# Four units' values in one run of 64 matmuls over five PSUM banks, in a fused attention and feed-forward kernel

## The chip, the cores and the metric

One core of a Trainium2 chip runs the kernel. The metric is the device time of one execution in microseconds (us), the median of several runs.

## What is computed

Sliding-window attention over 8 batches of 8 heads, 576 positions and 64 values a head: each position sees those at most 32 away. Its result, 4608 rows of 512, goes through a feed-forward layer with a sigmoid GELU.

```python
scores = (1 / sqrt(D)) * q @ k.T            # per batch and head
mask = abs(pos[:, None] - pos[None, :]) <= 32
attn = softmax(where(mask, scores, -1e9))
x = (attn @ v).transpose(0, 2, 1, 3).reshape(4608, 512)
h = x @ w_in                                # 512 -> 2048
out = (h * sigmoid(1.702 * h)) @ w_out      # 2048 -> 512
```

## The kernel before

**Units and tiles.** The 4608 rows are 36 units of 128 rows; four units make a tile of 512 rows, so there are 9 tiles. A unit holds two blocks of 64 queries. Its scores are computed transposed (keys in partitions), exponentiated on ScalarE into `p`, and multiplied by a mask of ones and zeros (`band`, L303) on VectorE. `values` (L311) multiplies `p` by V: for each of 8 heads and 2 blocks one matmul with 64 columns of `p` as weights and 65 columns of V, the last of them ones, so that the row sum comes out beside the 64 values. The two blocks of a head go to the lower and upper 64 partitions. The V of the first block lies in `ve`, that of the second in `vo`, the same rows moved by 64 partitions, which GpSimd copies (`odd_v`, L213, two copies a unit). `norm` (L330) takes the reciprocals of the row sums and multiplies, out of PSUM into `x`; `x_T` (L344) transposes `x` into `xT`, by a DMA that SP issues, or by TensorE through PSUM where a tag is given.

**PSUM.** There are eight banks: `A`, `C`, `B`, `E`, `LA`, `LB`, and `t`, which is two. A unit's values take either `t` (one reciprocal and one product on VectorE for eight heads) or `A` and `C` (one each for four heads and four).

**The feed-forward layer** is computed with seven half-size products a layer instead of eight (Winograd's form of Strassen's scheme), so sums of `xT`, of the weights and of `g` (`x_sums`, `w1_sums`, `g_sums`) are formed on VectorE. A tile's first layer is four groups (`l1_group`, L459); each issues P1, P7, P6, P2, P5, P4 and P3 of four 256-wide matmuls, over banks A, C, B and E. Between them ScalarE copies A to B and C to an SBUF tile, VectorE adds B and that tile into E (L484, after P6) and into C (L490, after P5), and ScalarE applies the GELU (L471). P5 and P3 add into B, so they wait until the addition before them has read it. Because P4 adds onto what VectorE has written in E, all of that bank must have been written by TensorE before.

**The order is written out by hand.** Each engine runs its instructions in the order in which the program issues them. The second layer of the tile before is a list of single matmuls, `l2`, and `do(l2, n)` issues the next n as fillers; a group's fillers stand after P1, P7, P2 and P4, as many as `SHARES` gives in that order (`fill`). Some of them carry an addition or a copy on VectorE or ScalarE behind them, and every 56th a store. `side` issues one piece of VectorE's waiting list `dv` after each of the two additions of a group, and `fill(4)` the rest of the list.

**One tile.** `front(t)` (L757) issues the scores of the next tile's four units in two pairs, with 20 fillers between and 12 behind. `back(t)` (L785) issues the four groups n = 0 to 3. Ahead of a group come `turn` (L748: two DMA transposes of q and k on SP), `fetch` (L736: loads of q, k and V on the queue of GpSimd, called POOL) and `spread` (L744: the `vo` copies of a later unit). Before the change, groups 1 and 3 begin with values: a unit in A and C, then one in `t`, with their `norm` and `x_T`, and a few fillers (`AHEAD`). Two masks are issued in group 0, two in group 1, and the sums of `g` of a group one group later. Tile 2 has an order of its own, with four runs of 16 value matmuls; in tile 7 unit 34 is transposed on TensorE in the last `front`.

Of the kernel before, what the change touches and what calls it, by code (L numbers as in the profile page):

```python
# [15 lines left out]
F32 = mybir.dt.float32  # L16
BF16 = mybir.dt.bfloat16
F16 = mybir.dt.float16
# [8 lines left out]
class _Kernel:  # L27
# [55 lines left out]
    def setup(self):  # L83
        nc, cst = self.nc, self.cst
        self.ident = cst.tile([128, 128], BF16, name="ident")
        self.identh = cst.tile([128, 128], F16, name="identh")
        self.mask = cst.tile([128, 4, SQ], BF16, name="mask")
        self.bias = cst.tile([128, 512], BF16, name="bias")
        self.w1 = cst.tile([128, 4, self.DFF], F16, name="w1")
        self.w2 = cst.tile([128, 16, self.DM], F16, name="w2")  # L90
        self.a = {i: cst.tile([128, 2, 1024], F16, name=f"a{i}") for i in (1, 2, 3, 4)}
        self.b = {i: cst.tile([128, 8, 256], F16, name=f"b{i}") for i in (1, 2, 3, 4)}
        self.k_first = cst.tile([128, 4, 64], BF16, name="k_first")
        self.v_first = cst.tile([64, self.H, 66], BF16, name="v_first")
        self.ve = [cst.tile([128, self.H, 66], BF16, name=f"ve{i}") for i in range(9)]
        self.vo = [cst.tile([128, self.H, 66], BF16, name=f"vo{i}") for i in range(5)]
        self.spark = cst.tile([128, 1], F32, name="spark")

    def setup_mask(self):
# [106 lines left out]
    def load_v(self, u, which=slice(None)):  # L206
# [3 lines left out]
        for off, b, s, n in list(self.pieces(128 * u, 128))[which]:  # L210
            self.nc.gpsimd.dma_start(t[off:off + n, :, :self.D], self.v[b, :, s:s + n, :].rearrange("h s d -> s h d"))  # L211

    def odd_v(self, u, eng, parts=(0, 1)):  # L213

        vo = self.vo[u % (3 if u > 15 else 5)]
        nxt = self.v_first if u == self.NU - 1 else self.ve[(u + 1) % 9][0:64]

        def words(ap):
            return ap.rearrange("p h d -> p (h d)").bitcast(I32)

        for i in parts:
            eng.tensor_copy(*((words(vo[64:128]), words(self.ve[u % 9][64:128])), (words(vo[0:64]), words(nxt)))[i])  # L222
# [88 lines left out]
    def values(self, u, tag):  # L311

        D = self.D
        p = self.p.pop(u)
        if tag == "t":
            acc = self.bank(tag, name="pv")
            self.acc[u] = [acc]
            acc = [acc[:, 0], acc[:, 1]]
        else:
            acc = [self.bank(x, name="pv") for x in tag]  # L320
            self.acc[u] = [x.rearrange("p (b n) -> p b n", b=1) for x in acc]
        for h in range(self.H):
            o = slice((h % 4) * (D + 1), (h % 4 + 1) * (D + 1))
            for blk in range(2):
                vt = (self.ve[u % 9], self.vo[u % (3 if u > 15 else 5)])[blk]
                w = p[:, h % 2, h // 2 * 2 + blk, :] if len(p.shape) == 4 else p[:, h % 2, h // 4, h // 2 % 2, blk, :]
                self.mm(acc[h // 4][64 * blk:64 * blk + 64, o], w, vt[:, h, :D + 1],
                        start=(h % 4 == 0))

    def norm(self, u):  # L330
        dve, D = self.nc.vector, self.D
        x = self.x[u] = self.sb("x", [128, self.H, D], F16, 4)
        rec = self.sb("rec", [128, 2, 4, 1], F32, 3)
        at = 0
        for acc in self.acc.pop(u):
            n = acc.shape[1]
            acc = acc[:, :, 0:4 * (D + 1)].rearrange("p b (h e) -> p b h e", e=D + 1)
            r = rec[:, at:at + n]
            dve.reciprocal(r, acc[:, :, :, D:])
            dve.tensor_mul(x[:, 4 * at:4 * (at + n), :].rearrange("p (b h) d -> p b h d", b=n), acc[:, :, :, :D],  # L340
                           r.to_broadcast([128, n, 4, D]))
            at += n

    def x_T(self, u, tag=None, eng=None):  # L344
        nc = self.nc
        t, s = divmod(u, 4)
        if t not in self.xT:
            self.xT[t] = self.sb("xT", [128, 4, TILE], F16, 2)
        x = self.x.pop(u).rearrange("p h d -> p (h d)")
        out = self.xT[t][:, :, 128 * s:128 * s + 128]  # L350
        if tag is None:
            nc.sync.dma_start_transpose(out, x)
            return
        tp = self.bank(tag, [128, 4, 128], F16, "tp")
        for c in range(4):
            nc.tensor.transpose(tp[:, c, :], x[:, 128 * c:128 * c + 128], self.identh)  # L356
        self.copy(eng, out, tp)
# [186 lines left out]
    def layer2(self, pairs, last):  # L544
# [54 lines left out]
        for P in (6, 2, 4, 5, 3):  # L599
# [3 lines left out]

    SHARES = {("first", 1): (3, 0, 5, 4), ("first", 2): (0, 6, 6, 6), ("first", 3): (3, 1, 7, 7), ("last", 0): (0, 12, 6, 6),
              0: (4, 4, 6, 6), 1: (3, 3, 6, 6), 2: (0, 6, 5, 6), 3: (2, 2, 5, 5)}


    AHEAD = {1: (0, 6), 3: (2, 3)}  # L610

    def opening(self):

# [138 lines left out]
    @staticmethod  # L752
    def do(fs, n=99):
        for _ in range(min(n, len(fs))):
            fs.pop(0)()

    def front(self, t, late):  # L757

        l2, do = self.l2, self.do
        if t + 1 == self.NT:  # L760
            self.l2eng = self.nc.scalar
            do(late, 3)
            do(l2, 8)
            self.x_T(self.NU - 2, "t", self.l2eng)
            xs = self.x_sums(t)
            do(xs, 1)
            do(l2, 12)
            do(late)
            do(xs)
            return  # L770
        self.l2eng = self.nc.vector
        u = 4 * t + 4
        self.scores(u, "t")
        self.scores(u + 1, "AC")
        do(late, 2)
        do(l2, 20)
        do(late)
        xs = self.x_sums(t)
        do(xs, 1)
        self.scores(u + 2, "BE")  # L780
        self.scores(u + 3, "t")
        do(l2, 12)
        do(xs)

    def back(self, t):  # L785

        more = t + 1 < self.NT
        do, l2 = self.do, self.l2
        u = 4 * t + 4
        bands = [lambda i=i: self.band(u + i) for i in range(4)] if more else []  # L790
        dv = bands[0:2]
        for n in range(4):
            if (t, n) == (3, 1):
                self.turn(20)
            if (t, n) != (3, 0):
                self.turn(u + n + 4)
            if (t, n) not in ((2, 3), (3, 0), (3, 3)):
                self.fetch(u + n + 5)
            if t == 2 and n in (1, 3):
                self.values(u + n - 1, "t")  # L800
                self.norm(u + n - 1)
                self.x_T(u + n - 1)
            elif more and n in (1, 3):
                do(l2, self.AHEAD[n][0])
                self.values(u + n - 1, "AC")
                self.norm(u + n - 1)
                if u + n < self.NU - 1:
                    self.x_T(u + n - 1)
                self.values(u + n, "t")
                self.norm(u + n)  # L810
                self.x_T(u + n)
                do(l2, self.AHEAD[n][1])
            if (t, n) == (3, 0):
                self.fetch(20)
            self.spread(u + n + 2)
            if (t, n) == (3, 0):
                self.fetch(21)
            if (t, n) == (3, 3):
                self.fetch(24)

            key = ("first", n) if t == 2 else ("last", n) if not more else n
            share = dict(zip((1, 7, 2, 4), self.SHARES.get(key, (3, 3, 5, 5))))

            def fill(i):
                do(l2, share[i])
                self.l2eng = self.nc.scalar
                if t == 2 and n in (1, 3) and i == 7:
                    self.values(u + n, "t")
                    if n == 3:
                        self.norm(u + n)  # L830
                        self.x_T(u + n)
                if i == 4:
                    do(dv, 2 if (t, n) == (2, 2) else 99)

            def side(i):
                if (t, n, i) == (2, 1, 0):
                    self.norm(u + n)
                    self.x_T(u + n)
                else:
                    do(dv, 1)  # L840

            self.l1_group(t, n, fill, side)
            dv += bands[2:4] if n == int(t == 2) else []
            dv += self.g_sums(t, 2 * n, 2)
        return dv

# [131 lines left out]
```

## Time and profile before

| | |
|---|---|
| median of 3 runs (range) | 281.47 us (281.16 to 281.52) |
| the profiled execution | 281.27 us, of which its span 279.5 us |
| TensorE busy | 268.2 us (96% of the span) |
| VectorE busy | 210.9 us (75%) |
| ScalarE busy | 195.4 us (70%) |
| GpSimd busy | 133.0 us (48%) |
| granted TensorE clock | 0.999 |

The page calls TensorE PE, VectorE DVE, ScalarE ACT, GpSimd POOL, and the queue that issues DMAs SP. A row of a timeline gives the start in us from the span's start, the time from the first start to the last end, the engine, the source line, the operation, what is written and read, and how many instructions the row merges; in brackets stands idle time before it and what ended it. Matmuls overlap, so the cost of one is read from start to start, not from its duration.

### The profile page before, as it was taken

The numbers are of one execution on the slowest core, as the hardware profiler recorded it, in microseconds if no ns is written. First come the engines' busy times: TensorE is split into PE (matmuls) and PEld (weight loads), VectorE is DVE, ScalarE is ACT, GpSimd is POOL, SyncE is SP. The second block draws the span as 40 slices with busy tenths as digits, with TensorE's granted clock in tenths as the row PEclk, the third lists the DMA queues.
The fourth block names the chain that finished last, engine by engine and source line by source line (L and its number), as shares of the span: only waits on it lengthen the run. The fifth ranks groups of instructions, "written<-read, shape, count | busy, mean of one in ns | idle before, by whom it ended". The sixth has DMA issues, their size and how long they took to land.

```text
span 279.5 us, 8854 instructions
## 1 busy us (share of the span) xinstructions
PE 268.2 (96%) x3632; PEld 222.6 (80%) x3632; DVE 210.9 (75%) x491; ACT 195.4 (70%) x343; POOL 133.0 (48%) x199
## 2 busy tenths in 40 slices
PE   1989999999999999999999999999999999999995
PEld 1568656776888888888888888888888888888884
DVE  3454598897997798788888887888778887945731
ACT  2586893989897588758875877687759775568411
POOL 8894695999593554635684519442520100000000
PEclk9999999999999999999999999999999999999999
DMA  8999999999999999999999999999972050202023
GB/s 88 166 204 199 178 207 165 185 136 159 131 167 140 203 120 140 172 189 115 182 194 178 126 163 159 134 183 132 168 91 85 2 115 19 77 2 75 2 104 124
DMA packets 150265, 37.61 MB, mean 135 GB/s; under 512 B 138064, under 2 KB 145872, under 8 KB 150224
## 3 DMA queue, kind: packets, MB, share of 16 engines
q0 software_dynamic: 106656, 18.42, 95.5%
q1 hardware_dynamic: 43120, 18.10, 37.9%
q8 instruction: 28, 0.46, 0.7%
q10 hardware_dynamic: 448, 0.52, 0.6%
q14 instruction: 13, 0.11, 0.1%
HBM read 36.83 MB, written 9.44 MB: 166 GB/s over the span
## 4 chain that ended last, share of the span: by engine, by line
PE 90%; DMA 4%; POOL 3%; ACT 1%; issue 1%; POOLq 0%
PE o L70 41%; PE h L70 39%; PE pv L70 4%; DMA w<-in_moe_w_in_dram 4%; PE sc L70 3%; POOL ve L211 1%; POOL kq L152 1%; PE tp L201 1%; PE tp L244 1%; ACT p L279 1%; POOL w L125 1%; PE tp L368 0%; ACT kq L67 0%; PE tp L356 0%; ACT L692 0%
## 5 line engine op out<-in xcount | busy, mean ns | idle before, releaser
L471 ACT ACTIVATE g<-h 128x512 f16<-128x512 f32 x128 | 72.2, 598 | 35.0 <-PE h L70 34.8
L222 POOL COPY vo<-ve 64x264 int32<-64x264 int32 x71 | 32.7, 461 | 79.3 <-PE pv L70 52.0
L70 PEld LDWEIGHTS <-g 128*128 128x128 f16 x576 | 54.5, 98 | 10.1
L70 PE MATMUL h<-xs,a 128*128 128x256 f16 x384 | 57.6, 272 | 0.0
L70 PEld LDWEIGHTS <-a 128*128 128x128 f16 x512 | 49.5, 98 | 9.1
L70 PE MATMUL o<-w,g 128*128 128x256 f16 (+1 forms) x320 | 55.0, 294 | 0.0
L70 PEld LDWEIGHTS <-w 128*128 128x128 f16 x496 | 47.7, 98 | 7.6 <-DMA w<-in_moe_w_in_dram 0.2
L70 PE MATMUL h<-xT,w 128*128 128x256 f16 (+1 forms) x368 | 53.5, 277 | 0.1
L70 PEld LDWEIGHTS <-gs 128*128 128x128 f16 x384 | 36.7, 98 | 4.7
L70 PE MATMUL o<-b,g 128*128 128x256 f16 x256 | 38.3, 273 | 0.0
L70 PE MATMUL o<-b,gs 128*128 128x256 f16 x256 | 37.7, 273 | 0.0
L484 DVE TENSOR_TENSOR h<-h,s 128x512 f32<-128x512 f32 x32 | 22.4, 699 | 19.8 <-PE h L70 19.1
L211 POOL DMA_DIRECT2D ve<-in_v_dram x40 | 34.3, 864 | 5.6 <-DMA w<-in_moe_w_out_dram 2.1
L279 ACT ACTIVATE p<-sc 128x512 bf16<-128x512 f32 x64 | 32.8, 618 | 1.2 <-PE sc L70 1.0
L67 ACT COPY h<-h 128x512 f32<-128x512 f32 x32 | 18.8, 588 | 16.7 <-PE h L70 16.3
L340 DVE TENSOR_TENSOR x<-pv,rec 128x256 f16<-128x256 f32 (+1 forms) x52 | 27.4, 527 | 1.8
L141 POOL DMA_DIRECT2D qst<-in_q_dram x35 | 28.2, 809 | 0.3
L490 DVE TENSOR_TENSOR h<-h,s 128x512 f32<-128x512 f32 x32 | 22.4, 699 | 6.4 <-PE h L70 6.1
L141 POOL DMA_DIRECT2D kst<-in_k_dram x31 | 26.5, 855 | 0.8 <-DMA w<-in_moe_w_out_dram 0.8
L309 DVE TENSOR_TENSOR p<-p,mask 128x1024 bf16<-128x1024 bf16 x32 | 22.3, 696 | 0.2
L67 ACT COPY s<-h 128x512 f32<-128x512 f32 x32 | 19.2, 600 | 1.2
L70 PE MATMUL h<-xs,w 128*128 128x256 f16 x128 | 19.2, 273 | 0.0
(88 smaller groups left out, 343.2 us busy)
## 6 DMA issues: line engine op xcount, KB each, us to landing
out_dram<-o_sb SPq DMA_DIRECT2D x33, 256.0 KB, 4.6
ve<-in_v_dram POOLq DMA_DIRECT2D x32, 128.0 KB, 6.9
kst<-in_k_dram POOLq DMA_DIRECT2D x25, 128.0 KB, 6.5
qst<-in_q_dram POOLq DMA_DIRECT2D x21, 128.0 KB, 5.6
w<-in_moe_w_out_dram POOLq DMA_DIRECT2D x4, 512.0 KB, 11.0
w<-in_moe_w_in_dram POOLq DMA_DIRECT2D x3, 512.0 KB, 9.9
qst<-in_q_dram POOLq DMA_DIRECT2D x7, 96.0 KB, 5.7
kq<-in_q_dram POOLq DMA_DIRECT2D x2, 256.0 KB, 5.9
```

The lines of the kernel that those rows point to most:

```text
L67: (eng.copy if eng is self.nc.scalar else eng.tensor_copy)(out, in_)
L70: self.nc.tensor.matmul(out, lhsT, rhs, start=start, stop=stop, skip_group_check=True)
L125: self.nc.gpsimd.dma_start(self.w1[:, :, lo:lo + n], self.w_in[:, lo:lo + n].rearrange("(k p) f -> p k f", p=128))
L141: self.nc.gpsimd.dma_start(t[off:off + n], src[b, :, s:s + n, :].rearrange("h s d -> s h d"))
L211: self.nc.gpsimd.dma_start(t[off:off + n, :, :self.D], self.v[b, :, s:s + n, :].rearrange("h s d -> s h d"))
L222: eng.tensor_copy(*((words(vo[64:128]), words(self.ve[u % 9][64:128])), (words(vo[0:64]), words(nxt)))[i])
L279: self.nc.scalar.activation(p[:, eo].rearrange("k h s -> k (h s)"), sc[eo], AF.Exp, scale=self.scale)
L309: (eng or self.nc.vector).tensor_mul(pv, pv, msk.to_broadcast([128, 8, 2, SQ]))
L340: dve.tensor_mul(x[:, 4 * at:4 * (at + n), :].rearrange("p (b h) d -> p b h d", b=n), acc[:, :, :, :D], r.to_broadcast([128, n, 4, D]))
L471: act.activation(g[:, f, 256 * half:256 * half + 256], bank.rearrange("p (i n) -> p i n", i=2), AF.Gelu_apprx_sigmoid)
L484: dve.tensor_add(e, b, s7)
L490: dve.tensor_add(c, b, s7)
```

## The change

The four units of a tile are multiplied by V in one run at the start of group 2 (`values_four`). The 32 heads of the four units are laid one behind the other: seven into A, four into C, fourteen into the two banks of `t`, seven into E. E is filled from its end, and the first matmul of each half is 57 columns wider, so that the whole bank is written. `norm_four` then takes one reciprocal and one product for each of the four pieces, and issues the DMA transpose of each unit as soon as it is whole. `x` becomes one tile for four units (`xn`).

What stands around it moves: all four masks are issued in group 0 (two by `side`, two by `fill(4)`); the sums of `g` of group 0 are split in group 1, two ahead of P6 and one behind each addition; group 2 has nothing behind its first addition. The fillers are distributed anew (80 a tile as before, 64 in tile 2). `vo` has four buffers in rotation from unit 16 on instead of three. In tile 2, fetch 19 and turn 19 come a group sooner, and its order is that of the other tiles; unit 34 is no longer transposed on TensorE.

```diff
-        vo = self.vo[u % (3 if u > 15 else 5)]
+        vo = self.odd(u)                  # self.vo[u % 5 if u < 16 else (2, 3, 4, 0)[u % 4]]
...
+    FOUR = (("A", 0, 7), ("C", 7, 4), ("t", 11, 14), ("E", 25, 7))
+    def values_four(self, u):
+        D = self.D
+        p = [self.p.pop(u + i) for i in range(4)]
+        for tag, lo, n in self.FOUR:
+            acc = self.acc[u, tag] = self.bank(tag, name="pv")
+            b = [acc[:, i] for i in range(2)] if tag == "t" else [acc]
+            pad = 512 - 7 * (D + 1) if tag == "E" else 0
+            for i in range(n):
+                x, h = divmod(lo + i, self.H)
+                at, more = pad + i % 7 * (D + 1), pad * (i == 0)
+                for blk in range(2):
+                    vt = (self.ve[(u + x) % 9], self.odd(u + x))[blk].rearrange("p h d -> p (h d)")
+                    self.mm(b[i // 7][64 * blk:64 * blk + 64, at - more:at + D + 1], p[x][:, h % 2, h // 2 * 2 + blk, :],
+                            vt[:, h * (D + 2) - more:h * (D + 2) + D + 1], start=(i % 7 == 0))
+    def norm_four(self, u):
+        dve, D = self.nc.vector, self.D
+        x = self.xn.rearrange("p u h d -> p (u h) d")
+        done = 0
+        for tag, lo, n in self.FOUR:
+            m, at = min(n, 7), 512 - 7 * (D + 1) if tag == "E" else 0
+            acc = self.acc.pop((u, tag))
...
+            r = self.sb("rec4", [128, 2, 7, 1], F32, 3)[:, 0:n // m, 0:m]
+            dve.reciprocal(r, acc[:, :, :, D:])
+            dve.tensor_mul(x[:, lo:lo + n].rearrange("p (b h) d -> p b h d", b=n // m), acc[:, :, :, :D],
+                           r.to_broadcast([128, n // m, m, D]))
+            while 8 * (done + 1) <= lo + n:
+                self.x[u + done] = self.xn[:, done]
+                self.x_T(u + done)
+                done += 1
...
-    SHARES = {("first", 1): (3, 0, 5, 4), ("first", 2): (0, 6, 6, 6), ("first", 3): (3, 1, 7, 7), ("last", 0): (0, 12, 6, 6),
-              0: (4, 4, 6, 6), 1: (3, 3, 6, 6), 2: (0, 6, 5, 6), 3: (2, 2, 5, 5)}
-    AHEAD = {1: (0, 6), 3: (2, 3)}
+    SHARES = {("first", 0): (3, 3, 4, 4), ("first", 1): (3, 3, 4, 4), ("last", 0): (0, 12, 6, 6),
+              0: (4, 5, 6, 7), 1: (4, 5, 6, 7), 2: (2, 4, 4, 5), 3: (4, 5, 5, 6)}
...                                         # front, last tile
-            self.x_T(self.NU - 2, "t", self.l2eng)
...                                         # back
-        dv = bands[0:2]
+        dv = bands
...
+            if (t, n) == (2, 2):
+                self.turn(19)
...
+            if (t, n) == (2, 1):
+                self.fetch(19)
-            if t == 2 and n in (1, 3):
-                self.values(u + n - 1, "t")
-                self.norm(u + n - 1)
-                self.x_T(u + n - 1)
-            elif more and n in (1, 3):
-                do(l2, self.AHEAD[n][0])
-                self.values(u + n - 1, "AC")
...
+            if more and n == 2:
+                self.values_four(u)
+                self.norm_four(u)
+                do(l2, 1)
...
-                if i == 4:
-                    do(dv, 2 if (t, n) == (2, 2) else 99)
+                if i == 4 or more and (n, i) == (1, 7):
+                    do(dv, 99 if i == 4 else 2)
...
-                if (t, n, i) == (2, 1, 0):
-                    self.norm(u + n)
-                    self.x_T(u + n)
-                else:
+                if not (more and n == 2 and i == 0):
                     do(dv, 1)
             self.l1_group(t, n, fill, side)
-            dv += bands[2:4] if n == int(t == 2) else []
             dv += self.g_sums(t, 2 * n, 2)
```

More of the change, by code (lines that the diff above doesn't have):

```diff
@@ L96, in setup @@
         self.vo = [cst.tile([128, self.H, 66], BF16, name=f"vo{i}") for i in range(5)]
+        self.xn = cst.tile([128, 4, self.H, self.D], F16, name="xn")
         self.spark = cst.tile([128, 1], F32, name="spark")
@@ L211, in load_v, with odd @@
             self.nc.gpsimd.dma_start(t[off:off + n, :, :self.D], self.v[b, :, s:s + n, :].rearrange("h s d -> s h d"))
+    def odd(self, u):
+        return self.vo[u % 5 if u < 16 else (2, 3, 4, 0)[u % 4]]
     def odd_v(self, u, eng, parts=(0, 1)):
-        vo = self.vo[u % (3 if u > 15 else 5)]
+        vo = self.odd(u)
         nxt = self.v_first if u == self.NU - 1 else self.ve[(u + 1) % 9][0:64]
@@ L324, in values @@
             for blk in range(2):
-                vt = (self.ve[u % 9], self.vo[u % (3 if u > 15 else 5)])[blk]
+                vt = (self.ve[u % 9], self.odd(u))[blk]
                 w = p[:, h % 2, h // 2 * 2 + blk, :] if len(p.shape) == 4 else p[:, h % 2, h // 4, h // 2 % 2, blk, :]
@@ L331, in norm @@
         dve, D = self.nc.vector, self.D
-        x = self.x[u] = self.sb("x", [128, self.H, D], F16, 4)
+        x = self.x[u] = self.xn[:, u % 4]
         rec = self.sb("rec", [128, 2, 4, 1], F32, 3)
@@ L342, in norm @@
             at += n
+    FOUR = (("A", 0, 7), ("C", 7, 4), ("t", 11, 14), ("E", 25, 7))
[20 more added lines that the diff above has]
+            acc = self.acc.pop((u, tag))
+            if tag != "t":
+                acc = acc.rearrange("p (b n) -> p b n", b=1)
+            acc = acc[:, :, at:at + m * (D + 1)].rearrange("p b (h e) -> p b h e", e=D + 1)
+            r = self.sb("rec4", [128, 2, 7, 1], F32, 3)[:, 0:n // m, 0:m]
[6 more added lines that the diff above has]
+                done += 1
     def x_T(self, u, tag=None, eng=None):
@@ L794, in back @@
                 self.turn(20)
-            if (t, n) != (3, 0):
+            if (t, n) not in ((2, 3), (3, 0)):
                 self.turn(u + n + 4)
-            if (t, n) not in ((2, 3), (3, 0), (3, 3)):
+            if (t, n) == (2, 2):
+                self.turn(19)
+            if (t, n) not in ((2, 2), (2, 3), (3, 0), (3, 3)):
                 self.fetch(u + n + 5)
-            if t == 2 and n in (1, 3):
-                self.values(u + n - 1, "t")
-                self.norm(u + n - 1)
-                self.x_T(u + n - 1)
-            elif more and n in (1, 3):
-                do(l2, self.AHEAD[n][0])
-                self.values(u + n - 1, "AC")
[L806 to L809, printed above, removed]
-                self.norm(u + n)
-                self.x_T(u + n)
-                do(l2, self.AHEAD[n][1])
+            if (t, n) == (2, 1):
[4 more added lines that the diff above has]
+                do(l2, 1)
             if (t, n) == (3, 0):
@@ L819, in back @@
                 self.fetch(24)
-            key = ("first", n) if t == 2 else ("last", n) if not more else n
+            key = n if more else ("last", n)
+            if t == 2:
+                key = ("first", n) if n < 2 else n
             share = dict(zip((1, 7, 2, 4), self.SHARES.get(key, (3, 3, 5, 5))))
@@ L826, in fill @@
                 self.l2eng = self.nc.scalar
[L827 to L831, printed above, removed]
-                if i == 4:
-                    do(dv, 2 if (t, n) == (2, 2) else 99)
+                if i == 4 or more and (n, i) == (1, 7):
+                    do(dv, 99 if i == 4 else 2)
             def side(i):
-                if (t, n, i) == (2, 1, 0):
-                    self.norm(u + n)
-                    self.x_T(u + n)
-                else:
+                if not (more and n == 2 and i == 0):
                     do(dv, 1)
             self.l1_group(t, n, fill, side)
-            dv += bands[2:4] if n == int(t == 2) else []
             dv += self.g_sums(t, 2 * n, 2)
```

## The prediction

> **What bounds the kernel now.** I read the page first, then the chain that ended last, then the timelines of TensorE, VectorE and the SP queue over one tile, then the landing times of the transposes.
>
> ```profile
> span 279.5 us, 8854 instructions
> ...
> PE 90%; DMA 4%; POOL 3%; ACT 1%; issue 1%; POOLq 0%
> ```
>
> The profiled execution took 281.27 us: its span of 279.5 and 1.77 around it. The median of the three runs, 281.47, lies 0.20 above it. Differences are worked out on the former and added to the latter. 90% of the chain is TensorE, so only what shortens or stops its stream counts. Its timeline in tile 4 shows how little there is to take:
>
> ```profile
> 137.70 0.60 PE L70 MATMUL h<-xT,a 128*128 128x256 f16 x4
> ...
> 138.89 0.83 PE L70 MATMUL o<-w,g 128*128 128x256 f16 x6
> 139.55 0.60 PE L70 MATMUL h<-xT,w 128*128 128x256 f16 x4
> ...
> 149.53 0.38 PE L70 MATMUL o<-b,g 128*128 128x256 f16 x2
> ...
> 150.61 0.50 PE L70 MATMUL o<-b,g 128*128 128x256 f16 x3
> ```
>
> From 138.89 to 139.55 six matmuls start, so a 256-wide matmul costs 0.109 us. Two runs of 32 value matmuls lie in the gaps: from 137.70 + 4 x 0.109 = 138.14 to 138.89 is 0.75, and from 149.53 + 2 x 0.109 = 149.75 to 150.61 is 0.86. Together 1.61 us of a tile.
>
> **The run of 64.** Tile 2 has four runs of 16 instead, of which two consecutive rows (value rows between them left out) show the price:
>
> ```profile
> 83.30 0.60 PE L70 MATMUL h<-xT,a 128*128 128x256 f16 x4
> ...
> 84.21 0.61 PE L70 MATMUL h<-xT,w 128*128 128x256 f16 x4
> ```
>
> 84.21 - 83.30 - 0.44 = 0.47 for 16. So 16 further value matmuls cost 0.75 - 0.47 = 0.28, 0.0175 each, and the rest is the price of entering and leaving. One run of 64 is 0.75 + 32 x 0.0175 = 1.31; the two padded matmuls (122 columns for 65) add at most their share of a second matmul each, I take 0.03: 1.34. If nothing waited, a tile would gain 0.27.
>
> **What VectorE does after it.** All four normalisations now stand in front of group 2's first addition (E = B + s7), on one in-order engine:
>
> ```profile
> 138.59 0.18 DVE L339 RECIPROCAL rec<-pv 128x4 f32<-128x4 f32 x1 [0.16 <-PE pv L70]
> 138.81 0.42 DVE L340 TENSOR_TENSOR x<-pv,rec 128x256 f16<-128x256 f32 x1
> 139.15 0.17 DVE L339 RECIPROCAL rec<-pv 128x4 f32<-128x4 f32 x1
> 139.36 0.43 DVE L340 TENSOR_TENSOR x<-pv,rec 128x256 f16<-128x256 f32 x1
> 139.70 0.20 DVE L339 RECIPROCAL rec<-pv 128x8 f32<-128x8 f32 x1
> 139.93 0.69 DVE L340 TENSOR_TENSOR x<-pv,rec 128x512 f16<-128x512 f32 x1
> ```
>
> Start to start a reciprocal of 4 costs 0.21, of 8 0.23; a product of 256 costs 0.34 (it lasts 0.42), and 512 lasts 0.27 longer, 1.04 ns an element. So 448 wide costs 0.54, 896 wide 1.01, and reciprocals of 7 and 14 some 0.23 and 0.27. The new order A (7 heads), C (4), t (14), E (7) is 0.23 + 0.54 + 0.21 + 0.34 + 0.27 + 1.01 + 0.23 + 0.54 = 3.37 us. Two units take 1.95 now (138.59 to 139.93 + 0.61); twice that less two reciprocals (0.42) and the fixed 0.07 of two products is 3.34, so the slope holds together. With whole durations it would be 3.54, the bound above.
>
> Call the first value matmul V. The first reciprocal began 0.36 after V (138.23) for 8 matmuls; for 14 it is 0.46. VectorE is then free at V + 0.46 + 3.37 = 3.83. What the addition costs TensorE is seen in group 2 now:
>
> ```profile
> 146.10 0.60 PE L70 MATMUL h<-xs,a 128*128 128x256 f16 x4
> ...
> 147.56 0.60 PE L70 MATMUL h<-xs,a 128*128 128x256 f16 x4
> ```
> ```profile
> 146.81 0.70 DVE L484 TENSOR_TENSOR h<-h,s 128x512 f32<-128x512 f32 x1
> ```
>
> P6 starts at 146.10, the addition 0.71 later, lasts 0.70, and P5, which adds into the bank that it reads, starts 0.05 behind it: 1.46 at least, where P6, P2 and 5 fillers give 13 x 0.109 = 1.42. So 0.04 is lost now, in group 3 likewise; the tile loses 1.61 + 0.08 = 1.69 to values and these waits.
>
> After the change P5 of group 2 can start at V + 3.83 + 0.70 + 0.05 = 4.58. TensorE would be there at V + 1.25 (the run less its 0.09 of entry) + 27 matmuls (1 filler, P1 4, 2, P7 4, 4, P6 4, P2 4, 4) x 0.109 = 4.20. It waits 0.38. P1 needs only A's product and is not late (V + 1.37). With group 3's 0.04 (5 fillers) the tile loses 1.34 + 0.38 + 0.04 = 1.76, against 1.69: **+0.07, five tiles +0.35**. The 0.27 of the longer run is eaten by the longer normalisation.
>
> The Trainium skill says on the page TensorEngine Tiling (Array Packing), section PSUM Bottleneck, that tiling speeds up TensorE and not the emptying of PSUM, which may then bind; by it the run's gain goes as above, and without it a tile would gain 0.31 instead.
>
> Tile 2 loses 4 x 0.47 = 1.88 and some such waits (0 to 0.3) now; after it 1.76 and, in its groups 0 and 1 with 4 fillers (12 x 0.109 = 1.31 for 1.46), 0.15 each: 2.06, and perhaps as much again behind P5. I take +0.1 (-0.1 to +0.4). Unit 34's transposes leave TensorE before the last tile:
>
> ```profile
> 239.36 0.39 PE L356 MATMUL tp<-identh,x 128*128 128x128 f16 x4
> 239.58 0.60 PE L70 MATMUL o<-w,gs 128*128 128x256 f16 x4
> ```
>
> That is **-0.22**. So far +0.35 + 0.1 - 0.22 = **+0.23**.
>
> **At nothing:** masks and sums of g only change place on VectorE. In group 0 three masks now follow the second addition:
>
> ```profile
> L309 DVE TENSOR_TENSOR p<-p,mask 128x1024 bf16<-128x1024 bf16 x32 | 22.3, 696 | 0.2
> ```
>
> Counted from start to start, 0.08 less than they last, that addition, the masks, a quarter's output and two sums of g take 0.62 + 3 x 0.61 + 0.34 + 0.8 = 3.6 us from P5's end, 4.2 from its start; group 1's addition waits for P6, 36 matmuls later, and 0.71: 4.6. That hides them by 0.4 us; without it the excess is paid, at most 0.5 a tile. Fetch 19 keeps its place among POOL's instructions. The copies into vo wait for TensorE less with four buffers:
>
> ```profile
> POOL vo L222 <- PE pv L70: 52.0, 11, 14.1
> ```
>
> This idle time is on no chain. What comes next is the landing of V, and loads that go out sooner, beside the transposes.
>
> **What is moved on SP.** Four x transposes now go out together in group 2, ahead of the last q and k transposes of the tile (group 3's turn). Now:
>
> ```profile
> 143.25 0.81 SPq L505 DMA_DIRECT2D out_dram<-o_sb  x2
> 144.16 1.44 SPq L235 DMA_TRANSPOSE qT<-qst  x1
> 145.70 1.73 SPq L235 DMA_TRANSPOSE kT<-kst  x1
> 147.54 1.26 SPq L235 DMA_TRANSPOSE qT<-qst  x1
> 148.90 1.21 SPq L235 DMA_TRANSPOSE kT<-kst  x1
> 151.42 2.54 SPq L352 DMA_TRANSPOSE xT<-x  x2
> ```
>
> After the change the store of group 1 goes out about V - 1.4 (its last matmul is 20 before the run, then a copy), the next transposes at V - 0.5, and one follows another every 1.3 to 1.6 us (1.27 for the pair of x, 1.58 on average over 144.16 to 148.90), say 1.4: q, k, four x, q, k. The last, k of the next tile's last unit, starts at V - 0.5 + 7 x 1.4 = V + 9.3. It lands so long after:
>
> ```profile
> L235 SPq DMA_TRANSPOSE kT<-kst x18: 1192/1266/1992, 82.0 to 192.8; - x18
> ...
> DMA to landing us min/median/max: 2.4/6.0/8.8
> ```
>
> The median gives V + 15.3. The scores that read it come in the next front:
>
> ```profile
> 156.36 2.29 PE o L70 x20
> 158.65 0.63 PE sc L70 x32
> ```
>
> From P5 at V + 4.58: 17 matmuls (1.86), group 3's 48 (5.24) and 0.04, 0.09 and 0.63 for two units' scores, 2.29 for 20 fillers and 0.3 for the unit before: V + 15.0. So TensorE waits **0.33**, and everything on it is queued behind. Bounds: a landing of 5 costs nothing; one of 7.0, the median of two k transposes that went out among loads in tile 4 (131.8 to 137 us), costs 1.3.
>
> ```profile
> kT<-kst SPq DMA_TRANSPOSE x2, 7.0
> ```
>
> I take the median of the same kind. This happens behind tiles 3, 4 and 5: in tile 2 the change puts turn 19 ahead of the x transposes, and behind tile 6 there is no next k and the loads are over. 3 x 0.33 = **+1.0**. There the x transposes have two more, 2.8 us, before them; the sums of x that read them come some 14.7 us after V, the last goes out by V + 9.3 and lands about V + 15.3, where VectorE would wait first, TensorE only if that wait outlasts the 12 fillers and P1 (1.7 us): I take nothing, at most 0.5 once. The sum is +0.23 + 1.0 = +1.2: 282.5 beside the profiled 281.27, and **282.7** beside the median.
>
> **The rivals.** *The transposes land in time.* Until now the last k starts at 148.90 and is read at 158.9, 10 us later; then it has 5.7, and it misses by a third of a microsecond in my sum; a spacing of 1.3 alone wins 0.7. Then +0.23: 281.7, within the noise. Against it: x transposes and loads sooner share the engines.
>
> *VectorE does not bind the run (faster).* If the normalisation took 0.3 us less, or E's part did not stand before the addition, P5 would be held only by its own 1.46: 1.25 + 15 x 0.109 + 1.46 = V + 4.35, 0.23 sooner in six tiles: 0.23 - 1.4 = -1.2, 280.3. It decides once the chain is below 3.1. For it: the products of 448 and 896 stand in no row. Against it: their slope does.
>
> *Every VectorE instruction costs its whole duration.* The rows show the next one starting 0.08 before a product's end. If the wide ones with their reciprocals did not overlap, the chain would be 3.54, P5 0.17 later in six tiles: 0.23 + 1.0, 282.7. The Trainium skill, VectorE: DVE Perf Modes, section The DRAIN you can't avoid, says the next operation cannot issue until the pipeline is empty; the rows (0.34 from start to start for 0.42) speak against counting it so.
>
> **How the numbers follow.** About 0.2% (0.56 us) is what a measurement of this kernel can tell from no change. Late transposes have 0.46 (slower); transposes in time 0.28 (within); VectorE not binding 0.20 (faster); whole durations 0.06 (slower). Faster 0.20, within 0.28, slower 0.52. The forecast's own range is 282.0 to 285.6 (landings of 5.8 to 7.0). Leaving out the faster half of the faster case and the last of the late one, the range is 280.4 to 284.8.
>
> **What would show it.** In the changed profile: one run of 64 value matmuls a tile, about 1.3 us with its edges; the first DVE L484-type addition of group 2 about 3.8 after V with no idle time before it, and P5 at V + 4.6; TensorE stopping before the second unit of the second pair of scores behind tiles 3 to 5, released by the DMA of kT or qT; no x transposes on TensorE behind tile 7. I am wrong if the scores never wait (then 281.7), or if P5 starts right behind its fillers (then faster).

## The result, and the profile after

| | before | after |
|---|---|---|
| median (range), 6 runs each | 281.50 us (280.77 to 283.48) | 290.97 us (290.51 to 293.71) |
| profiled execution, its span | 281.27, 279.5 us | 291.84, 290.1 us |
| granted TensorE clock | 0.999 | 0.988 |

The change makes the kernel slower: the ratio is 1.034 (95% interval 1.029 to 1.039). The forecast, 282.7 us, had the direction and the place, not the size: its range ended at 284.8. The span grew by 10.6 us.

The page of after: the granted clock in 40 slices (tenths of full speed), and the chain that ended last, by engine and by line.

```profile
PEclk9999999999999999997799999999999999999999
...
PE 78%; DMA 13%; POOL 3%; DVE 2%; ACT 1%; issue 1%; DVEq 0%; POOLq 0%
```

DMA has 13% of the chain where it had 4%, and two slices in the middle have a lower clock; before, all forty read 9. The waits of TensorE (line, what it waited for: us in total, times, longest) name the DMA:

```profile
PE h L70 <- DVE h L526: 2.5, 6, 0.4
PE sc L70 <- DMA qT<-qst: 2.4, 1, 2.4
PE sc L70 <- DMA kT<-kst: 2.2, 3, 1.1
```

None of the three was there before. L526 is group 2's first addition, seen six times, once a run of 64. The other two are the scores behind tiles 3, 4 and 5. TensorE's timeline at these three fronts:

```profile
132.10 0.45 PE L70 MATMUL sc<-qT,kT 64*64 64x64 bf16 x24
134.97 0.31 PE L70 MATMUL sc<-qT,kT 64*64 64x64 bf16 x2 [2.43 <-DMA qT<-qst]
135.65 0.64 PE L70 MATMUL sc<-qT,kT 64*64 64x64 bf16 x22 [0.36 <-DMA kT<-kst]
136.22 1.89 PE L70 MATMUL o<-b,gs 128*128 128x256 f16 x8
137.90 1.06 PE L70 MATMUL o<-w,g 128*128 128x256 f16 x4
...
141.31 0.72 PE L70 MATMUL o<-b,g 128*128 128x256 f16 x5
...
165.97 0.48 PE L70 MATMUL sc<-qT,kT 64*64 64x64 bf16 x26
...
167.90 0.83 PE L70 MATMUL o<-b,gs 128*128 128x256 f16 x6
...
195.17 0.48 PE L70 MATMUL sc<-qT,kT 64*64 64x64 bf16 x26
...
196.73 0.72 PE L70 MATMUL o<-b,gs 128*128 128x256 f16 x5
```

The second pair of scores took 0.63 us before. Here it takes 136.22 - 132.10 = 4.12, then 1.93 and 1.56: 3.49, 1.30 and 0.93 us too long, **5.7 in all**. Behind the first of them the matmuls are slow: eight in 137.90 - 136.22 = 1.68 us, 0.21 each where 0.109 is the rule. The windows view (length, busy time of each engine, granted clock) of that stretch:

```profile
136.20:141.30 5.10, 5.10 (x28) 3.63 (x25) 2.03 (x5) 1.66 (x3) 2.22 (x3) 0.50 2.24 183
```

A clock of 0.50 for 5.1 us (from 132.0 to 136.2 it is 0.80 on average, so it falls at about 136.2 - 2 x 0.20 x 4.2 = 134.5, within the stop): 24 matmuls from 136.22 to 141.31 cost 5.09 us in place of 2.62, **2.5 us** more. This split is that of the profiled execution: over the six, the granted clock lies between 0.988 and 0.998. The remaining 10.6 - 5.7 - 2.5 = **2.4 us** are spread over the tiles; the largest part of them is a longer wait at P5 of group 2. VectorE in tile 3:

```profile
117.61 0.21 DVE L378 RECIPROCAL rec<-pv 128x7 f32<-128x7 f32 x1
117.86 0.62 DVE L379 TENSOR_TENSOR xn<-pv,rec 128x448 f16<-128x448 f32 x1
118.40 0.17 DVE L378 RECIPROCAL rec<-pv 128x4 f32<-128x4 f32 x1
...
119.21 1.09 DVE L379 TENSOR_TENSOR xn<-pv,rec 128x896 f16<-128x896 f32 x1
120.22 0.20 DVE L378 RECIPROCAL rec<-pv 128x7 f32<-128x7 f32 x1
120.45 0.62 DVE L379 TENSOR_TENSOR xn<-pv,rec 128x448 f16<-128x448 f32 x1
121.21 0.70 DVE L526 TENSOR_TENSOR h<-h,s 128x512 f32<-128x512 f32 x1
```

and TensorE there (the first value matmul, V, started at 117.16; the rows between are left out):

```profile
116.63 0.60 PE L70 MATMUL h<-xT,a 128*128 128x256 f16 x4
...
118.33 0.28 PE L70 MATMUL o<-b,gs 128*128 128x256 f16 x1
118.54 0.61 PE L70 MATMUL h<-xT,w 128*128 128x256 f16 x4
...
121.06 0.49 PE L70 MATMUL o<-w,g 128*128 128x256 f16 x3
121.96 0.60 PE L70 MATMUL h<-xs,a 128*128 128x256 f16 x4 [0.41 <-DVE h L526]
```

The run costs 118.33 - 116.63 - 0.44 = 1.26 us with its edges. P1 starts 0.21 behind one filler, so it waits 0.10. P5 starts at 121.96, where TensorE was done with its fillers at 121.06 + 3 x 0.109 = 121.39: it waits 0.57. (The 0.41 in the row is counted from the end of the last matmul, which lies past its slot.)

### The profile page after: what moved, and what is told of

It is laid out like the page before. It is cut to its first block, busy times and chain, and to the rows that moved or that the text cites. A ratio compares the mean times of both kernels' runs of the same rounds, so it can differ in the third digit from the quotient of the medians.

```text
span 290.1 us, 8830 instructions
## 1 busy us (share of the span) xinstructions
PE 270.7 (93%) x3628; PEld 224.0 (77%) x3628; DVE 210.6 (73%) x471; ACT 196.5 (68%) x342; POOL 133.0 (46%) x199
## 4 chain that ended last, share of the span: by engine, by line
PE 78%; DMA 13%; POOL 3%; DVE 2%; ACT 1%; issue 1%; DVEq 0%; POOLq 0%
PE h L70 36%; PE o L70 34%; DMA kT<-kst 8%; PE pv L70 3%; DMA w<-in_moe_w_in_dram 3%; DMA xT<-xn 2%; PE sc L70 2%; DVE h L526 1%; POOL ve L212 1%; POOL kq L153 1%; PE tp L202 1%; PE tp L248 1%; ACT p L283 1%; POOL w L126 1%; PE tp L410 0%
## 5 line engine op out<-in xcount | busy, mean ns | idle before, releaser
L70 PEld LDWEIGHTS <-g 128*128 128x128 f16 x576 | 55.8, 99 | 10.4
L70 PE MATMUL o<-w,g 128*128 128x256 f16 (+1 forms) x320 | 56.7, 298 | 0.0
L70 PE MATMUL o<-b,gs 128*128 128x256 f16 x256 | 40.7, 278 | 0.0
L526 DVE TENSOR_TENSOR h<-h,s 128x512 f32<-128x512 f32 x32 | 22.4, 699 | 21.1 <-PE h L70 19.5
L70 PE MATMUL o<-b,g 128*128 128x256 f16 x256 | 36.3, 273 | 0.0
L67 ACT COPY h<-h 128x512 f32<-128x512 f32 x32 | 18.5, 578 | 16.2 <-PE h L70 15.7
L313 DVE TENSOR_TENSOR p<-p,mask 128x1024 bf16<-128x1024 bf16 x32 | 21.4, 685 | 0.3 <-ACT p L283 0.3
L67 ACT COPY o_sb<-o 128x256 f32<-128x256 f32 (+1 forms) x23 | 10.7, 467 | 12.6 <-PE o L70 12.6
```

The lines of the kernel that those rows point to most:

```text
L67: (eng.copy if eng is self.nc.scalar else eng.tensor_copy)(out, in_)
L70: self.nc.tensor.matmul(out, lhsT, rhs, start=start, stop=stop, skip_group_check=True)
L313: (eng or self.nc.vector).tensor_mul(pv, pv, msk.to_broadcast([128, 8, 2, SQ]))
L526: dve.tensor_add(e, b, s7)
```

## Experiments

Two things could make the transposes late: the **order** on SP (the last two of q and k now go out behind four of x) and **crowding** (loads that GpSimd issues sooner, now that `vo` has four buffers, run beside them). And P5's longer wait could come from the length of VectorE's chain or from the addition waiting for E. Each kernel ran in alternation with the kernel before on one chip; ratios are to that. Kernels that share an edit name the one on which they stand.

**The turn first.** The changed kernel; the last turn of the tile goes out in group 2, ahead of the x transposes:

```diff
-            if (t, n) not in ((2, 3), (3, 0)):
+            if (t, n) != (3, 0) and not (more and n == 3):
                 self.turn(u + n + 4)
...
+            if more and n == 2:
+                self.turn(u + 7)
             if more and n == 2:
                 self.values_four(u)
```

> The changed kernel, but each tile's last two q and k transposes (group 3's turn) go out on SP ahead of the four x transposes instead of behind them. Theory A (the order on SP makes the next tile's scores wait, and the pause of 3.5 us in tile 4 halves TensorE's clock for some 5 us): the waits of 3.49, 1.30 and 0.93 us before the scores and the 2.5 us of slow matmuls all go, 290.97 - 8.2 = 282.8 us, granted clock 0.999. Theory B (loads that go out sooner and the x transposes crowd the DMA engines, whatever the order): the transposes still land late, waits of 1 us and more remain, 286 us or more.

Measured: 284.28 us, ratio 1.0075 (1.0042 to 1.0109). The scores behind the tile run through, and the clock is 0.998:

```profile
131.08 0.70 PE L70 MATMUL sc<-qT,kT 64*64 64x64 bf16 x48
131.71 1.05 PE L70 MATMUL o<-b,gs 128*128 128x256 f16 x8
```

The 48 take 0.63 again. So the order is needed for the late scores, and both they and the slow clock go with it. The six waits at P5 stay. By its ratio it is some 0.8 us slower than expected (1.0075 for 282.8 / 281.5 = 1.0046); a stop of 0.6 us before P1 of tile 4, where x, now last on SP, comes late, is part of that.

**The order alone.** The kernel before; from tile 3 on, group 3's turn goes out behind the x transposes of that group:

```diff
-            if (t, n) != (3, 0):
+            late = t > 2 and more and n == 3
+            if (t, n) != (3, 0) and not late:
                 self.turn(u + n + 4)
...
                 do(l2, self.AHEAD[n][1])
+            if late:
+                self.turn(u + 7)
```

> The kernel before, with one thing of the change alone: from tile 3 on, group 3's turn goes out on SP behind that group's two x transposes instead of ahead of them. Theory A: the last k transpose starts some 4 us later than now, lands about 160 instead of 154 us in tile 4, and the scores that read it (about 159) wait 0.5 to 1.5 us behind tiles 3 to 5: 283 to 286 us. Theory B: without the four x transposes in a row and without sooner loads nothing is late, 281.5 us.

Measured: 302.0 us, ratio 1.0675 (1.0593 to 1.0758), far more than expected. Its waits of TensorE, and the clock of one of three such stretches of 6.8 us:

```profile
PE sc L70 <- DMA qT<-qst: 7.8, 3, 3.5
PE sc L70 <- DMA kT<-kst: 5.0, 3, 1.8
```
```profile
134.80:141.60 6.80, 5.16 (x45) 3.71 (x46) 1.61 (x4) 1.66 (x3) 1.89 (x3) 0.50 1.92 191
```

The new order, with the loads issued when they were before, is enough to make the scores wait, here longer than in the changed kernel, since in group 3 the x transposes themselves wait for the values: the k transpose starts at 128.13 for scores at 131.2. What I undershot is how fast the price grows: a stop of this length brings the half clock.

This run does not separate order from crowding, though. GpSimd issues six loads from 123.69 to 128.96 us here, as it does before (123.74 to 129.01). Before, the last k transpose of the tile left at 121.17, ahead of them; here it leaves at 128.13, behind them. It lands so long after, before and here:

```profile
kT<-kst SPq DMA_TRANSPOSE x1, 4.3
```
```profile
kT<-kst SPq DMA_TRANSPOSE x1, 8.6
```

Moving a transpose back on SP thus made it later twice: it left 7 us later, and it stood among loads that had not moved.

**E ahead of t.** The kernel with the turn first, and E's seven heads are filled and normalised before t's fourteen, whose normalisation goes behind group 2's second addition:

```diff
-    FOUR = (("A", 0, 7), ("C", 7, 4), ("t", 11, 14), ("E", 25, 7))
+    FOUR = (("A", 0, 7), ("C", 7, 4), ("E", 11, 7), ("t", 18, 14))
...
-                self.norm_four(u)
+                self.norm_four(u, "ACE")
...
+                if more and (n, i) == (2, 1):
+                    self.norm_four(u, "t")
```

> As e1, and E is filled and normalised before t; t's normalisation is issued behind group 2's second addition instead of ahead of the first. Theory C (P5 of group 2 waits 0.58 us because the first addition writes E and so stands behind the whole chain of four normalisations, and does not overlap E's product): the addition starts 0.71 after P6, P5 waits 0.15 (4 fillers instead of 5.4), six tiles save 0.43 each: 2.6 us less than e1, about 280.2. Rival D (the addition is held by P2, after whose last matmul it also started): P5 still waits 0.5 or more, same as e1.

Measured: 281.94 us, ratio 0.9993 (0.9966 to 1.0021). VectorE and TensorE of that place:

```profile
119.54 0.70 DVE L528 TENSOR_TENSOR h<-h,s 128x512 f32<-128x512 f32 x1 [0.97 <-PE h L70]
```
```profile
119.83 0.49 PE L70 MATMUL o<-w,g 128*128 128x256 f16 x3
120.30 0.60 PE L70 MATMUL h<-xs,a 128*128 128x256 f16 x4
```

The addition now waits for P6 and not for VectorE, and P5 starts 0.47 after the last three fillers started: it waits 0.14 in place of 0.57, six times, 2.6 us in sum, close to the 2.3 us that the median fell. VectorE's chain in front of the addition was the cause of these 0.43 us a tile; the 0.14 left is the addition waiting for P6. The rival that P2 holds the addition falls too: P2, started at 119.29, ran until 119.89.

**The fillers.** The kernel with E ahead of t, and the fillers moved to where 0.14, 0.10 and 0.04 were still lost:

```diff
-    SHARES = {("first", 0): (3, 3, 4, 4), ("first", 1): (3, 3, 4, 4), ...
-              0: (4, 5, 6, 7), 1: (4, 5, 6, 7), 2: (2, 4, 4, 5), 3: (4, 5, 5, 6)}
+    SHARES = {("first", 0): (2, 2, 5, 5), ("first", 1): (2, 2, 5, 5), ...
+              0: (4, 5, 6, 7), 1: (4, 5, 6, 7), 2: (2, 2, 6, 5), 3: (3, 4, 6, 6)}
...
-                do(l2, 1)
+                do(l2, 2)
```

> As e3, and the 36 fillers of groups 2 and 3 are dealt out so that 2 follow the run (instead of 1) and 6 stand between P2 and P5 in both groups (instead of 4 and 5); tile 2's groups 0 and 1 get 5 there and 5 behind P4 (instead of 4 and 4). By the arithmetic 'P5 can start 1.46 us, 13.4 matmuls, after P6' the waits of 0.14, 0.09 and 0.04 in six tiles go (1.6 us), and 0.35 in tile 2: about 1.9 us less than e3, 280.0 us, or 0.5% below the kernel before. If the fillers only move the wait to P3 or to the next group's P1, the time stays that of e3, 281.9.

Measured: 282.11 us (279.88 to 288.39), ratio 1.0002 (0.9971 to 1.0033): by its time, neither the gain nor its absence is shown. In the profiled execution (284.13 us) the small waits are gone, but TensorE stops once, for 2.7 us before P7 of tile 4's first group, for sums of x that wait for the x transposes; 3.4 us at half clock follow:

```profile
PE h L70 <- DVE xs L444: 2.8, 2, 2.5
```

So what is left there is x, last on SP with loads beside it. That its lateness changes from run to run fits the wide spread of the times, but only this execution has a profile.

**Without the late loads of V.** The changed kernel, turn not moved; V of the units from 22 on is not loaded, and an older V is multiplied instead:

```diff
-        elif u >= 18:
+        elif 18 <= u < 23:
             self.load_v(u - 1)
```

> The changed kernel without the loads of V from unit 22 on (those units' values are computed from old V): a third of the loads beside the transposes of tiles 4 and 5 is gone, the order on SP is the changed kernel's. Theory A (order alone): the last k transpose still starts some 10 us after the run of values and lands 5 to 6 us later: waits of about 0.3 to 1 us before the scores stay, 3 us in all, 287 to 289 us. Theory B (crowding): waits behind tiles 4 and 5 vanish, 284 to 286 us.

Measured: 288.24 us, ratio 1.0217 (1.0146 to 1.0289). The scores behind tile 3 stop for 2.0 us in place of 3.5, behind tile 4 not at all, behind tile 5 for 0.9 (the rows of the first stand in the last section).

With a third of the loads gone, half of the waiting goes. So crowding has a share in it, and the order another: behind tile 3 the last k goes out 5.7 us before it is read in place of 4.9, and lands after 7.6 us in place of 8.1. As this kernel also moves less data altogether, it does not settle the shares.

**Loads staggered, turn first.** The fillers' kernel; from tile 4 on the `vo` copies of group 0 go ahead of its loads on GpSimd, which holds the loads back until V has landed:

```diff
+            if n == 0 and t > 3:
+                self.spread(u + 2)
             if (t, n) not in ((2, 2), (2, 3), (3, 0), (3, 3)):
                 self.fetch(u + n + 5)
...
-            self.spread(u + n + 2)
+            if n > 0 or t < 4:
+                self.spread(u + n + 2)
```

> As e4, and from tile 4 on GpSimd copies vo before it issues group 0's loads, so that these go out some 6 us later, when the copies' V has landed, and not among the transposes that follow the run. If loads crowd the transposes of x (whose landing made VectorE wait up to 1.5 us and TensorE's P1 0.6 us in e1 and e3), that wait goes in the tiles from 5 on: up to 0.7 us less than e4. If not, the same as e4; if POOL now brings V late to the run, slower by a microsecond or more.

Measured: 278.93 us, ratio **0.991** (0.988 to 0.994): 0.9% faster than the kernel before. Its span is 277.2 us, DMA has 5% of its chain, and its waits of TensorE are those of the opening and of the last unit's transposes, which the kernel before has too: none for the transposes of a later tile, none at P5.

**Turns in group 1 instead.** The fillers' kernel; from tile 4 on the turns of groups 2 and 3 and a fetch go out in group 1:

```diff
+            if early and n == 1:
+                self.fetch(u + 7)
+                self.turn(u + 6)
...
-            if more and n == 2:
+            if more and n == (1 if early else 2):
                 self.turn(u + 7)
```

> As e4, and from tile 4 on the tile's last four q and k transposes go out on SP in group 1, ahead of the store there (which waits for ScalarE until some 1.4 us before the run), so that the x transposes are first on SP after the run. The x transposes then start up to 3 us sooner than in e1 and e3; if their queue place is what makes x late, no wait of TensorE before P1 remains in tiles 5 to 8: 0.7 us less than e4. If crowding alone does it, the same as e4.

Measured: 281.05 us, ratio 0.9973 (0.9949 to 0.9997). That interval overlaps the one of the fillers' kernel (0.9971 to 1.0033), so a gain from moving the turns is not shown. The one longer stop before P1 in its profile, 0.8 us, lies in tile 4, ahead of the place from which the edit acts. Moving the loads does gain: its interval lies below both.

**Loads staggered, order as in the change.** The changed kernel with the edit of `spread` above and nothing else:

> The changed kernel with one edit: from tile 4 on the vo copies of the unit that group 0 spreads are issued ahead of group 0's loads on GpSimd instead of behind them, so that those loads go out later; the order on SP stays as the change has it. Tile 3 is not touched, so the wait of 3.5 us before the scores behind it and the half clock that follows (together about 6 us) should stay, as a control within the run. Order theory: behind tiles 4 and 5 the last transposes start as late as before, so some wait remains even without crowding; by the half that stayed when V was not loaded I expect 0.3 to 0.7 of the 1.30 and 0.93 us, total 289.5 to 290.5. Crowding theory: loads out of the way bring the landing from about 8 back to 6 us and both waits go, total 288.8. Rival, neither: the waits stay at 1.30 and 0.93, 291.

Measured: 284.0 us, ratio 1.0062 (1.0026 to 1.0098): most of the loss is gone with the order untouched, against what I expected. The control was none: GpSimd runs ahead, so that the edit of tile 4's group 0 acts beside the transposes of tile 3. Its queue in the changed kernel, and here:

```profile
121.48 0.89 POOL L142 DMA_DIRECT2D qst<-in_q_dram  x1
...
125.83 0.92 POOL L212 DMA_DIRECT2D ve<-in_v_dram  x1
```
```profile
121.37 0.89 POOL L142 DMA_DIRECT2D qst<-in_q_dram  x1
...
123.12 0.89 POOL L212 DMA_DIRECT2D ve<-in_v_dram  x1
```

Six loads in 5.3 us there, three here and then none until 130.21. The last k transpose went out at nearly the same time (127.52 and 127.10) and landed so long after (median of the one issue, in the list of DMA issues of after, then of this kernel):

```profile
kT<-kst SPq DMA_TRANSPOSE x1, 8.1
```
```profile
kT<-kst SPq DMA_TRANSPOSE x1, 5.7
```

TensorE behind tile 3:

```profile
131.29 0.45 PE L70 MATMUL sc<-qT,kT 64*64 64x64 bf16 x24
...
133.21 1.05 PE L70 MATMUL o<-b,gs 128*128 128x256 f16 x8
```

The stop there shrinks from 3.49 to 133.21 - 131.29 - 0.63 = 1.29 us, no half clock follows, behind tile 4 there is none, and behind tile 5 it is 1.26. Within this one run, with one order, the landing follows the loads. Behind tile 4 no load went out from 149.6 to 155.3, and the last k (154.87) landed after 4.6 us. Behind tile 5 the edit did not hold the loads back: six went out from 181.85 to 187.1, and the last k (182.54) landed after 7.4. So with the loads out of the way the order costs 1.3 us at one front and nothing at another, where the forecast had 0.33 at each.

**Loads sooner, order and values as before.** The kernel before with the four `vo` buffers alone:

```diff
-        vo = self.vo[u % (3 if u > 15 else 5)]
+        vo = self.vo[u % 5 if u < 16 else (2, 3, 4, 0)[u % 4]]
```

> The kernel before with one edit: vo has four buffers in rotation instead of three, so that its copies and the loads queued behind them on GpSimd go out sooner; values, their order and the order on SP are those of before. Crowding theory: the loads then fall beside the transposes as in the changed kernel and a landing may take 8 us in place of 6, but with the old order the last k transpose has about 10 us until the scores read it, so no wait appears: 281.3 to 282.0. Rival: sooner loads alone make the scores wait (landings of over 10 us, or the q and k themselves arriving late): 283 or more. Other rival: sooner loads help by themselves, below 281.

Measured: 282.86 us, ratio 1.0031 (0.9993 to 1.0068). No wait before scores, as expected. Its profiled execution has one stop that I had not expected, in TensorE's timeline 134.37 - 132.25 - 3 x 0.109 = 1.79 us long:

```profile
132.25 0.49 PE L70 MATMUL o<-w,g 128*128 128x256 f16 x3
134.37 0.27 PE L70 MATMUL o<-w,g 128*128 128x256 f16 x1 [1.63 <-issue]
```

Beside it VectorE waits for x, ahead of an addition into the bank of the second layer:

```profile
133.33 0.43 DVE L400 TENSOR_TENSOR xs<-xT 128x512 f16<-128x512 f16 x1 [0.95 <-DMA xT<-x]
```

Put together, the two causes do not add:

| | loads as before or staggered | loads sooner |
|---|---|---|
| last turn ahead of x | 1 (before) | 1.003 (before, four `vo`); 1.0075 (change, turn first) |
| last turn behind x | 1.006 (change, staggered up to tile 4) | 1.034 (the change) |

Each alone stays under 1%, P5's waits in the two kernels of the change included; together they use up the slack, and the stop is then long enough to halve the clock. The kernel with the order alone (1.0675) stands outside the table: its k transposes go out 3.1 us before their scores (128.13 for 131.2), those of the change 4.9 (127.52 for 132.4), and they stand among loads that go out when they always did. What the runs point to is whether the last transposes stand beside loads and how soon they are read; how much of that in the change is due to the four `vo` buffers is not shown, since no run has the change with three.

## Why the prediction was right in direction and wrong in size

**The run of 64: right.** 1.26 us against 1.34.

**VectorE's chain: right to the hundredth.** The first reciprocal at V + 0.45 (0.46 predicted), 0.54 for 448 wide, 1.01 for 896. The rivals "VectorE does not bind" and "whole durations" fall here: from 117.61 to 120.45 + 0.54, the end of E's slot, the chain is 3.38 us for 3.37, and each product, the wide ones too, overlaps by 0.08 with the reciprocal behind it (118.40 for 117.86 + 0.62).

**The addition behind it: 0.22 late.** The sum let it start at V + 3.83; it started at V + 4.05. The last product ends at 120.45 + 0.62 = 121.07, and the addition starts 0.14 behind that end, where what follows the other products starts 0.08 ahead of theirs. It is the only one that writes what the one before it reads (E); that this is why is read from the rows alone, since the runs took the chain away as a whole. The Trainium skill (VectorE: DVE Perf Modes, The DRAIN you can't avoid) lets no operation start before the pipeline is empty, and adds that one which is not held starts earlier; of the four products' followers three agree with the second half and this one alone with the first. So P5 waited 0.57 in place of 0.38, six times: 1.2 us. P1, "not late", waited 0.10 a tile: 0.6 us. Where I had +0.23 for all that is not SP, it is +2.4; these two give 1.8 of the difference. Small stops in the opening, in tile 2 and in the first group of tile 3 (0.27 before P7, 0.13 before P6), less what the run saved, go the right way for the rest; they are not all accounted for.

**The order on SP: the place right, the term mis-sized.** The three fronts, the second unit of the second pair and the releasers are those predicted. SP's queue:

```profile
116.68 1.39 SPq L239 DMA_TRANSPOSE qT<-qst  x1
...
119.53 6.11 SPq L394 DMA_TRANSPOSE xT<-xn  x4
126.16 1.25 SPq L239 DMA_TRANSPOSE qT<-qst  x1
127.52 1.31 SPq L239 DMA_TRANSPOSE kT<-kst  x1
```

The first went out at V - 0.5, as said; the last at V + 10.4, not V + 9.3, since a transpose takes 1.55 us of the queue and not 1.4. It landed 8.1 us later, not 6.0: at V + 18.5 for V + 15.3. TensorE needed it at 132.10 + 0.31 = V + 15.25 (V + 15.0 predicted). The wait of 0.33 was the small difference of two large sums, and both errors went the same way: 1.1 + 2.1 us. **The step that failed is the landing time**: I took the median of all k transposes of the kernel before, 6.0, whether loads stood beside them or not, and the 7.0 of two among loads only as the bound; the row itself had 8.8 as its longest. The same part said that loads go out sooner, beside the transposes, and I put that at nothing. The runs show 8.1 us in the change and 8.6 with the order alone, behind six loads each, for 5.7 behind three (staggered) and 4.3 ahead of the six (before). So the late landing was the larger half of the error. It does not take sooner loads: with the order alone the loads had not moved.

The Trainium skill, DMA: Bandwidth & Descriptors, section Queues, rings and completion order, says that each DMA engine serves in turn, packet by packet, the queues that have work for it; so a transpose beside loads of another queue takes longer. The landings agree with that; no run shows the turns themselves.

**What was not in the sum at all: the half clock**, 2.5 us. The profile of before could have hinted at it in one place only, its opening, behind the 6.3 us that TensorE waits before its first matmul:

```profile
7.48 1.04 PE L70 MATMUL sc<-bias,ident 128*128 128x512 bf16 x2
...
13.45 0.81 PE L70 MATMUL sc<-bias,ident 128*128 128x512 bf16 x3 [0.15 <-DVE kq L67]
```

The next rows start at 8.45 and 14.19, so a matmul of 512 columns costs 0.49 us there and 0.25 six us later. The clock column reads 1.00 throughout, so it is not shown that this is the same half clock.

**At nothing, rightly:** masks, sums of g, fetch 19 and the turn of tile 2 appear in no wait; unit 34's transposes left TensorE.

## What to carry to other kernels

A wait that comes out as the small difference of a long chain and a long chain has an error as large as the chains': price it with the landing times of transfers that run beside what the change puts beside them, and not with the median of the undisturbed ones. Where an in-order queue carries transfers with different deadlines, send the one that is read first first, and look at what a freed buffer lets another queue issue at that time. A normalisation that must be done before an accumulation goes on belongs in front of those that need not.

## What the runs showed of the hardware

A stop of TensorE has a second price. Stops at one place that summed to 1.8 us or less (1.30 and 0.93 in the change, 1.29 and 1.26 with staggered loads, 1.79 in the kernel before with four `vo`) were followed by full speed. Those of 2.0 us (without the loads of V) and 2.7 (the fillers) came with 3.4 us at half clock, those of 3.5 (the change) and 4.0 to 5.8 (the order alone) with 6.8 us, begun within the stop or just behind it:

```profile
131.14 0.45 PE L70 MATMUL sc<-qT,kT 64*64 64x64 bf16 x24
...
133.77 1.14 PE L70 MATMUL o<-b,gs 128*128 128x256 f16 x8
134.71 1.06 PE L70 MATMUL o<-w,g 128*128 128x256 f16 x4
135.56 1.06 PE L70 MATMUL h<-xT,w 128*128 128x256 f16 x4
```

These rows are from the run without the loads of V: a stop of 133.77 - 131.14 - 0.63 = 2.0, and the matmuls behind it slow down: the eight from 133.77 take (134.71 - 133.77) / 8 = 0.12 us each, the next four 0.21. The Trainium skill, TensorE: Matmul & The Clock Gate, section HAM oscillation, puts the limit at idle gaps of about 3.4 us; here shorter ones did it, the 2.7 without a matmul in it, the 2.0 with two short ones. The half of the clock itself agrees (0.50). What exactly decides between 1.8 and 2.0 us stays open; no run varied the length of a stop by itself.
